# Outer products over all 128 rows and 512 columns, and a new order of the tail, in a decode backward kernel

## The chip, the cores and the metric

The kernel runs on one core of a Trainium2 chip. The metric is the device time of one execution in microseconds; the median of 11 runs of the kernel before is 517.34 us (510.51 to 527.18). Engines are named as in the profile: PE (matmul) and PEld (its weight loads), DVE (vector), ACT (scalar), POOL (GpSimd), SP (which here only issues loads and the two small row stores).

## The reference, cut to what matters

The forward pass is a residual block for one decoded token (batch 2): a layer norm, then grouped-query attention over a cached K and V next to a gated bilinear feed-forward block, both added to x. The kernel returns its output and, by the chain rule, the gradients of x, of both caches and of all weights.

```
x: (2, 1, 576)   k_cache, v_cache: (2, 16, 4096, 128)   wq: (576, 4096)   wo: (4096, 576)
w_gate, w_up: (576, 4608)   w_down: (4608, 576)          all bf16

q = xn @ wq                       # 32 query heads of 128, 2 to each of the 16 key heads
p = softmax(q k^T / sqrt(128));   o = p v;   attention = o @ wo
h = (xn @ w_gate) * (xn @ w_up);  feed-forward = h @ w_down
out = x + attention + feed-forward
returned: out and d/d(x, k_cache, v_cache, wq, wo, w_gate, w_up, w_down) of sum(out * grad_out)
```

The gradients of the caches are sums of two outer products (two query heads to a key head): dV[k, :] = sum over the two heads of p[k] times dO[:], and dK[k, :] the same with the score gradient ds[k] and q[:]. All weight gradients are sums of outer products over the batch of 2. So 92.5 MB are read and 92.5 MB are written, and almost no operand is used twice.

## The kernel before, in words

**Order of the work.** The outer loop has NIT = 16 iterations (L841 to L882): four groups of four key heads, in each group two batches and two pairs s of key heads. One iteration loads two K heads and two V heads (1 MB each) and makes the dV of its own pair and the dK of the pair of the iteration before, which is kept in `last` with its K tiles, its score gradients `dsT`, `dsm` and its queries `bd0`. Each head is one `slot` (L738): its load is issued on SP, then half of the head is transposed on DVE in 32x32 blocks (`t32`, L121, into one of three X tiles) and multiplied on PE by a stationary W (16 matmuls, `head_scores`, L519), then `more(2)` runs two waiting outer-product units, then comes the other half, two more units, and `other(per)`, which runs steps of the list `side`. `side` holds the feed-forward slices (9 slices of 512 columns, `mlp_units`) and, after the last pair of a group, the weight work of the group (`back_units`, L637). `contract` (L535) is the second use of a K or V head: its rows times the probabilities or the score gradients, with the result in `oT`; `end_of_K` and `end_of_V` (L749, L754) call it.

**Outer products of the caches.** `masked` (L557, POOL, 1.9 us) spreads a 128x128 array of probabilities or score gradients into `prm` or `dsm`, eight matrices [128, 128], each with the rows of one part left and the others at zero. `build_bd` (L497) makes the other factor: POOL copies a column of q or dO into the diagonal matrices dM, PE multiplies them by the identity, and ACT copies the result [128, 2 x 128] from PSUM to `bd0` or `bd1` in bf16. `outer_units` (L564) makes eight units of a pair of heads. A unit takes one PSUM tile `ps_o` of two banks (two such tiles exist), fills it with eight matmuls of 32 rows x 128 stationary columns on 128 moving columns, where `32 * a` picks a row strip, and copies its 1024 columns to a quarter of a store tile `so`. The fourth unit of a head issues the store of 1 MB on POOL's queue (L581).

**Who copies out of PSUM.** `evac` (L104) keeps two counters of microseconds, for DVE and ACT, adds its own estimate to the smaller one and so picks the engine; other work is added by hand through `dve()` and `act()`.

**Buffers.** Tag "nat": 12 slots for everything that is loaded (K, V, weights) and, at the end, for the small row tiles of `final_units`. Tag "st": 5 slots for all store tiles but two small ones. Tag "X": 3 slots. `ps_m`, small PSUM tiles: 2.

**The end.** After the loop, `end_of_K` of the last pair runs; then its eight dK units are added to `outs`, and `side` gets, in this order, the small row tiles (`prepare`), `first` (output rows `yp`, the 16 transposes of oT into R, the stationaries of the input gradient), `second` (`dxn`), the rows of out_0 (`output`), `rows` and `gradient` for dx, and then the weight gradients of the last group: `outer_o` (dWo: 8 copies of 576 columns, two stores of 576 KB), `outer_q` (dWq: 4 copies of 1024 columns, two stores of 512 KB) and `outer_qt`. The last loop alternates two dK or dV units with one entry of `side`.

PE runs its instructions in the order in which they were placed; within a `Block` all matmuls follow the first one directly (L83 to L100). The framework places the instructions by priority and adds the semaphores.

Of the kernel before, what the change touches and what calls it, by code (L numbers as in the profile page):

```python
# [11 lines left out]
FP32 = mybir.dt.float32  # L12
BF16 = mybir.dt.bfloat16
P = 128
# [9 lines left out]
def kernel(  # L24
# [201 lines left out]
    oTs = [const.tile([P, 2, GH, 32], BF16, name=f"oT{i}") for i in range(2)]  # L226
    for t in (*Wms, *Wts, *oTs):
        nc.gpsimd.memset(t[:], 0.0)
    nwm = [0]

    rowT = [[const.tile([P, P + 28], BF16, name=f"rowT{t}{i}") for i in range(2)] for t in range(2)]
# [211 lines left out]
    def group_front(g, wq, wo):  # L443
        qd = sb.tile([P, 3, GH, 2], BF16, tag="qd", bufs=2, name="qd")
        qp = ps_m([P, GH, 2])
        with Block() as mm:
            for h in range(GH):
                for dc in range(5):
                    if dc < 4:
                        l, r = wq[:, 2 * dc + h // 4, (h % 4) * P:(h % 4 + 1) * P], xs[:, dc, 0:2]  # L450
                    else:
                        l, r = wq[:, 8, (h % 4) * P:(h % 4 + 1) * P], xs[:, 4 + h // 4, 0:2]
                    mm(qp[:, h, :], lhsT=l, rhs=r, start=(dc == 0), stop=(dc == 4))
        nc.vector.tensor_copy(qd[:, 0], qp[:])
        nc.vector.tensor_scalar(qd[:, 2], qd[:, 0], SCALE, None, op0=ALU.mult)

        do_ps = ps_m([P, GH * 32])
        for half in range(2):
            Xo = xtile([P, GH // 2, D], "Xo")
            t32(pairs(Xo[:].rearrange("p c n -> p (c n)")),  # L460
                pairs(wo[:, 4 * half:4 * half + 4].rearrange("p c n -> p (c n)")))
            with Block() as mm:
                for k in range(NB):
                    for e in range(2):
                        mm(
                            do_ps[:, P * half:P * half + P], lhsT=Wdy[:, k, e, :],
                            rhs=view(Xo[:], 0, P, 64 * k + e, [[D, 4], [2, 32]]),
                            start=(k == 0 and e == 0), stop=(k == NB - 1 and e == 1),
                        )
        dof = sb.tile([P, GH, 32], FP32, tag="dof", bufs=1, name="dof")  # L470
        t32(dof[:].rearrange("p c n -> p (c n)"), do_ps[:])
        nc.vector.tensor_copy(qd[:, 1], dof[:, :, 0:2])


        rp = ps_m([P, 2, 4, GH * 2])
        for t in range(2):
            for be in range(4):
                nc.tensor.matmul(rp[:, t, be, :], lhsT=sel[:, be].rearrange("p a i -> p (a i)"),
                                 rhs=qd[:, t].rearrange("p h b -> p (h b)"), start=True, stop=True)
        rep = sb.tile([P, 2, 4, GH * 2], BF16, tag="rep", bufs=2, name="rep")  # L480
        nc.vector.tensor_copy(rep[:], rp[:])
        dve(2.6 + 1.2)
        return dict(g=g, wq=wq, wo=wo, qd=qd, rep=rep, oT=oTs[g % 2])
# [13 lines left out]
    def build_bd(st, b, s, t):  # L497

        nc.gpsimd.tensor_copy(  # L499
            view(dM[:], 0, P, t * 2 * P, [[P + 2, 2], [4, 32], [1, 2]]),  # L500
            view(st["qd"][:], 0, P, (2 if t == 0 else 1) * GH * 2 + 8 * s + b, [[4, 2], [0, 32], [2, 2]]),
        )
        bp = ps_m([P, 2, Dh])
        for x in range(2):
            nc.tensor.matmul(bp[:, x, :], lhsT=dM[:, t, x], rhs=ident[:], start=True, stop=True)  # L505
        bd = sb.tile([P, 2 * Dh], BF16, tag=f"bd{t}", bufs=2, name=f"bd{t}")
        nc.scalar.copy(bd[:], bp[:].rearrange("p x d -> p (x d)"))
        act(0.4)
        return bd

    def small(name, shape=(P, 1), dtype=FP32, bufs=2):
# [44 lines left out]

    def masked(rows, name):  # L557

        m = sb.tile([P, 8, P], BF16, tag=name, bufs=2, name=name)
        nc.gpsimd.tensor_tensor(m[:], view(rows[:], 0, P, 0, [[0, 8], [1, P]]),  # L560
                                view(maskc[:], 0, P, 0, [[1, 8], [0, P]]), ALU.mult)
        return m

    def outer_units(rows, bd, b, l0, oview):  # L564
        m = {}

        def unit(x, ch, A):
            def f():
                if ch == 0 and A == 0:
                    m["st"] = stile([P, 4, 8, Dh], "so")  # L570
                st = m["st"]
                o = ps_o()
                with Block() as mm:
                    for c in range(4):
                        for aa in range(2):
                            a = 2 * A + aa
                            mm(o[:, aa, c * Dh:(c + 1) * Dh], lhsT=rows[32 * a:32 * a + 32, 4 * ch + c, :],
                                             rhs=bd[32 * a:32 * a + 32, x * Dh:(x + 1) * Dh], start=True, stop=True)
                evac(st[:, 2 * A:2 * A + 2, 4 * ch:4 * ch + 4, :].rearrange("p a c d -> p a (c d)"), o[:], 1024)
                if ch == 1 and A == 1:  # L580
                    nc.gpsimd.dma_start(oview[b, :, :, l0 + x].rearrange("a m n -> m a n"),  # L581
                                        st[:].rearrange("p a c d -> p a (c d)"))
            return f
        return [unit(x, ch, A) for x in range(2) for ch in range(2) for A in range(2)]

    def softmax(s_ps):
        mx = small("mx")
# [49 lines left out]
    def back_units(st):  # L637
        g, wq, wo, oT = st["g"], st["wq"], st["wo"], st["oT"]
        n0 = g * GH * Dh
        m = {}  # L640

        def first():
            yp = ps_m([P, 5, 2])
            with Block() as mm:
                for dc in range(5):
                    for h in range(GH):
                        mm(yp[:, dc, :], lhsT=wo[:, h, DOFF[dc]:DOFF[dc] + P], rhs=oT[:, 0, h, 0:2],
                                         start=(h == 0), stop=(h == GH - 1))
            nc.vector.tensor_add(acc[:], acc[:], yp[:])

            rp = ps_m([P, 2, 2, P], BF16)
            for t in range(2):
                for h in range(GH):
                    a = h // 2
                    nc.tensor.transpose(rp[32 * a:32 * a + 32, t, h % 2, :], oT[:, t, h, :], ident[:])
            m["R"] = R = sb.tile([P, 2, 2, P], BF16, tag="R", bufs=1, name="R")
            nc.vector.tensor_copy(R[:], rp[:])
# [6 lines left out]
            dve(0.2 + 0.5)  # L664

        def second():
            dxn(*m["W"], wq, lambda q, s: (s // 4) * 16 + q * 4 + s % 4, lambda s: s // 4, 2)
# [1 line left out]
        def outer_q(k, A):  # L669
            def f():  # L670
                R = m["R"]
                if A == 0:
                    m["st"] = swtile([P, 2, GH * P], "stq")
                st = m["st"]
                o = ps_o()
                with Block() as mm:
                    for dc in range(2):
                        for aa in range(2):
                            a = 2 * A + aa
                            d0 = (2 * k + dc) * P  # L680
# [23 lines left out]
        def outer_o(A, h2, k):  # L704
            def f():
                R = m["R"]
                if h2 == 0 and k == 0:
                    m["so"] = swtile([P, 4, D], "sto")
                o = ps_o()
                with Block() as mm:  # L710
                    for aa in range(2):
# [6 lines left out]
                    nc.gpsimd.dma_start(out_5[r0:r0 + 4 * P, :].rearrange("(h p) n -> p h n", p=P), m["so"][:])  # L718
            return f

        return [[first], [second], [outer_o(0, 0, 0), outer_o(0, 0, 1)], [outer_o(0, 1, 0), outer_o(0, 1, 1)],
                [outer_o(1, 0, 0), outer_o(1, 0, 1)], [outer_o(1, 1, 0), outer_o(1, 1, 1)],
                [outer_q(0, 0), outer_q(0, 1)], [outer_q(1, 0), outer_q(1, 1)], [outer_qt]]

# [116 lines left out]
    for n in range(NIT):  # L841
# [38 lines left out]
        last = (st, b, s, K, dsT, dsm, bd0)  # L880
        if new:
            st = nxt  # L882
    end_of_K(*last[:5])
    outs += outer_units(last[5], last[6], last[1], G * last[0]["g"] + 2 * last[2], okview)
    units = back_units(last[0])
    side += final[:1] + units[:2] + final[1:] + units[2:]
    while outs or side:
        more(2)
        other(1)
# [30 lines left out]
```

## Time and profile before

| | us |
|---|---|
| median of 11 runs | 517.34 |
| the profiled execution, its own time | 517.05 |
| its span (first to last instruction) | 515.3 |
| PE / DVE / ACT / POOL busy | 422.0 / 353.9 / 332.3 / 201.8 |
| outer matmuls of the caches, 2048, mean 0.24 | 95.1 |
| score matmuls, 2048 | 164.4 |
| ACT copies ps_o to so, 232 of 256, mean 1.02 | 225.2 |
| DVE copies ps_o to so, 24, mean 1.20 | 28.8 |
| POOL masks, 32, mean 1.89 | 60.5 |
| DMA moved | 186.26 MB, 361 GB/s over the span |
| mean granted TensorE clock | 0.831 of full |

How to read it: busy times are per engine and overlap. [...] The page's clock line gives the granted TensorE clock in 40 slices of 12.9 us, in tenths of full speed, the DMA line the busy share of the 16 DMA engines.

### The profile page before, as it was taken

To read this page: it belongs to the slowest core of one execution; us is meant where nothing else is said; L and a number is where in the kernel's file an instruction comes from. 1 tells how busy PE (TensorE), PEld (TensorE's weight loads), DVE (VectorE), ACT (ScalarE), POOL (GpSimd) and SP (SyncE) were. 2 spreads that over 40 slices of the span, in tenths; PEclk is the share of its full clock that TensorE was granted. 3 is DMA by queue.
4 is the path that set the end of the run, shared out by engine and by line. 5 is a ranking of instruction groups with operands and counts; after the bars stand their busy time and mean duration, and the time that the engine had idled before them with its cause. 6 is when DMAs were issued, how large, how long until landed. Compare 5 with 4: busy or idle time off the path is not lost.

```text
span 515.3 us, 20060 instructions
## 1 busy us (share of the span) xinstructions
PE 422.0 (82%) x8921; PEld 338.0 (66%) x8921; DVE 353.9 (69%) x621; ACT 332.3 (64%) x461; POOL 201.8 (39%) x369
## 2 busy tenths in 40 slices
PE   2778997989988987983888889988987988799772
PEld 1667775867776666773677667776776766677630
DVE  6785765556748969563587678768684769598464
ACT  4244795657587486873477864768776475788553
POOL 3224363233352444440534435356243155353313
PEclk9797896577799699986799975889897599999655
DMA  8998999999979999998799999999999999976646
GB/s 257 405 383 315 399 381 386 385 335 390 370 278 406 410 341 415 408 406 347 274 402 398 414 416 396 364 396 417 419 414 392 419 374 379 390 270 234 245 191 238
DMA packets 52911, 186.26 MB, mean 361 GB/s; under 512 B 4140, under 2 KB 19128, under 8 KB 44632
## 3 DMA queue, kind: packets, MB, share of 16 engines
q1 hardware_dynamic: 28392, 92.49, 47.2%
q0 software_dynamic: 24432, 92.48, 45.5%
q8 instruction: 70, 1.15, 0.9%
q14 instruction: 17, 0.14, 0.1%
HBM read 92.48 MB, written 92.48 MB: 359 GB/s over the span
## 4 chain that ended last, share of the span: by engine, by line
PE 53%; ACT 16%; DVE 14%; issue 9%; DMA 4%; SPq 2%; POOL 1%; POOLq 0%; ACTq 0%; DVEq 0%
PE ps_sc L93 20%; PE ps_o L93 14%; ACT so L112 13%; PE ps_m L93 12%; DVE X L121 5%; DMA wd<-in_B_w_down_dram 2%; SPq L313 2%; PE ps_m L554 2%; DVE so L109 2%; DMA wgu<-in_B_w_gate_dram 2%; DVE Xw L121 1%; PE ps_m L603 1%; PE ps_m L625 1%; PE ps_m L505 1%; ACT stw L112 1%
## 5 line engine op out<-in xcount | busy, mean ns | idle before, releaser
L112 ACT CAST so<-ps_o 128x1024 bf16<-128x1024 f32 x232 | 225.2, 1021 | 71.9 <-PE ps_o L93 61.6
L121 DVE STREAM_TRANSPOSE X<-kv 128x1024 f32<-128x1024 f32 x128 | 157.6, 1234 | 51.0 <-PE ps_sc L93 45.6
L93 PE MATMUL ps_sc<-X,W 128*128 128x128 bf16 x2048 | 164.4, 240 | 14.4 <-issue 7.7
L93 PEld LDWEIGHTS <-W 128*128 128x128 bf16 x2048 | 145.9, 108 | 23.2 <-issue 17.4
L581 POOL DMA_DIRECT2D out_dram<-so x64 | 49.9, 779 | 119.2 <-ACT so L112 75.1
L93 PE MATMUL ps_o<-bd,dsm 32*128 32x128 bf16 x1024 | 49.7, 241 | 13.5 <-ACT so L112 9.0
L93 PE MATMUL ps_o<-bd,prm 32*128 32x128 bf16 x1024 | 45.4, 232 | 13.4 <-ACT so L112 5.8
L93 PEld LDWEIGHTS <-dsm 32*128 32x128 bf16 x1024 | 30.5, 102 | 28.4 <-issue 22.8
L93 PEld LDWEIGHTS <-prm 32*128 32x128 bf16 x1024 | 27.5, 98 | 26.1 <-issue 19.3
L93 PE MATMUL ps_m<-kv,rowT 128*32 128x128 bf16 x2048 | 40.8, 240 | 2.6 <-issue 2.0
L112 ACT CAST stw<-ps_o 128x1024 bf16<-128x1024 f32 x28 | 28.0, 1019 | 16.0 <-PE ps_o L93 14.4
L492 POOL COPY W<-rep 32x16 bf16<-32x16 bf16 x128 | 24.8, 194 | 34.1 <-PE ps_sc L93 27.0
L93 PEld LDWEIGHTS <-rowT 128*32 128x32 bf16 x2048 | 34.4, 108 | 5.0 <-issue 2.8
L560 POOL TENSOR_TENSOR prm<-pr,maskc 128x1024 bf16<-128x1024 bf16 x16 | 30.2, 1890 | 15.5 <-DVE pr L608 14.2
L560 POOL TENSOR_TENSOR dsm<-ds,maskc 128x1024 bf16<-128x1024 bf16 x16 | 30.3, 1894 | 9.1 <-DVE ds L628 8.6
L109 DVE CAST so<-ps_o 128x1024 bf16<-128x1024 f32 x24 | 28.8, 1198 | 4.4 <-PE ps_o L93 4.4
L499 POOL COPY dM<-qd 128x128 bf16<-128x128 bf16 x32 | 9.2, 291 | 47.5 <-PE ps_m L505 32.8
L121 DVE STREAM_TRANSPOSE Xw<-wgu 128x1152 f32<-128x1152 f32 x18 | 24.6, 1365 | 4.0 <-PE ps_sc L93 3.9
L112 ACT CAST std<-ps_o 128x576 bf16<-128x576 f32 x36 | 22.1, 646 | 5.9 <-PE ps_o L93 5.1
L112 ACT CAST sto<-ps_o 128x576 bf16<-128x576 f32 x25 | 15.1, 643 | 15.6 <-PE ps_o L93 15.6
L392 POOL DMA_DIRECT2D out_dram<-stw x18 | 13.7, 759 | 29.1 <-ACT stw L112 13.0
L93 PEld LDWEIGHTS <-Wdy 128*128 128x128 bf16 x306 | 22.0, 110 | 4.3 <-DVE Xo L121 2.9
(174 smaller groups left out, 544.5 us busy)
## 6 DMA issues: line engine op xcount, KB each, us to landing
out_dram<-so POOLq DMA_DIRECT2D x64, 1024.0 KB, 11.2
kv<-in_A_k_cache_dram SPq DMA_DIRECT2D x32, 1024.0 KB, 12.7
kv<-in_A_v_cache_dram SPq DMA_DIRECT2D x32, 1024.0 KB, 10.6
out_dram<-stw POOLq DMA_DIRECT2D x18, 512.0 KB, 11.0
wd<-in_B_w_down_dram SPq DMA_DIRECT2D x9, 576.0 KB, 11.3
out_dram<-std POOLq DMA_DIRECT2D x9, 576.0 KB, 8.7
wo<-in_A_wo_dram SPq DMA_DIRECT2D x4, 1152.0 KB, 15.3
wgu<-in_B_w_gate_dram SPq DMA_DIRECT2D x9, 512.0 KB, 17.9
```

The source lines that it names most:

```text
L93: ins = nc.tensor.matmul(*args, **kwargs)
L109: nc.vector.tensor_copy(out=out, in_=in_)
L112: nc.scalar.copy(out, in_)
L121: nc.vector.transpose(out, in_)
L313: nc.sync.dma_start(wgu[64 * w:64 * w + 64, 8], Wsrc[512:576, f0:f0 + FS])
L392: nc.gpsimd.dma_start(out[0:512, f0:f0 + FS].rearrange("(c p) n -> p c n", p=P), st[:])
L492: nc.gpsimd.tensor_copy(view(W[t][:], 32 * a, 32, 28 + 32 * a, [[2 * WW, 4], [WW + 2, 2], [1, 2]]), view(st["rep"][:], 32 * a, 32, t * 4 * ...
L499: nc.gpsimd.tensor_copy(view(dM[:], 0, P, t * 2 * P, [[P + 2, 2], [4, 32], [1, 2]]), view(st["qd"][:], 0, P, (2 if t == 0 else 1) * GH * 2 ...
L505: nc.tensor.matmul(bp[:, x, :], lhsT=dM[:, t, x], rhs=ident[:], start=True, stop=True)
L554: nc.tensor.matmul(t_ps[:], lhsT=o_sb[:], rhs=RV[:].rearrange("p x r -> p (x r)"), start=True, stop=True)
L560: nc.gpsimd.tensor_tensor(m[:], view(rows[:], 0, P, 0, [[0, 8], [1, P]]), view(maskc[:], 0, P, 0, [[1, 8], [0, P]]), ALU.mult)
L581: nc.gpsimd.dma_start(oview[b, :, :, l0 + x].rearrange("a m n -> m a n"), st[:].rearrange("p a c d -> p a (c d)"))
```

## The change

**The factor bd over all rows.** `build_bd` now copies the PSUM result on ACT to a tile `dense`, and POOL copies it, 32 partitions at a time, into the diagonal blocks of one of three permanent tiles `bds` of shape [128, 2, 4, 128], whose other blocks are set to zero once at the start. **The outer units** make 1024 columns in two matmuls of all 128 rows and 512 moving columns each, in place of eight of 32 rows and 128 columns; a unit now covers all four row strips of two of the eight matrices, so its copy writes runs of 128 columns into `so`. `prm` and `dsm` share a tag with three slots (before: two each), and `dof` moves to an X slot. **The tail**: `first` is cut into `output`, `turn(0)`, `turn(1)` and `spread`; the order of `side` changes; two dV units go ahead of the last `end_of_K`; the counters of `evac` restart at zero; the store tiles of the last group's dWo and dWq take "nat" slots.

```diff
+    bds = [const.tile([P, 2, 4, Dh], BF16, name=f"bd{i}") for i in range(3)]
+    for r in bds:
+        nc.gpsimd.memset(r[:], 0.0)
+    n_bd = [0]
...
-        dof = sb.tile([P, GH, 32], FP32, tag="dof", bufs=1, name="dof")
+        dof = sb.tile([P, GH, 32], FP32, tag="X", bufs=3, name="dof")
...
-        bd = sb.tile([P, 2 * Dh], BF16, tag=f"bd{t}", bufs=2, name=f"bd{t}")
-        nc.scalar.copy(bd[:], bp[:].rearrange("p x d -> p (x d)"))
+        dense = sb.tile([P, 2, Dh], BF16, tag="dense", bufs=1, name="dense")
+        nc.scalar.copy(dense[:], bp[:])
         act(0.4)
+        bd = bds[n_bd[0] % 3]
+        n_bd[0] += 1
+        for a in range(4):
+            nc.gpsimd.tensor_copy(bd[32 * a:32 * a + 32, :, a, :], dense[32 * a:32 * a + 32])
         return bd
...
-        m = sb.tile([P, 8, P], BF16, tag=name, bufs=2, name=name)
+        m = sb.tile([P, 8, P], BF16, tag="msk", bufs=3, name=name)
...
-        def unit(x, ch, A):
+        def unit(x, cp):
...
                 with Block() as mm:
-                    for c in range(4):
-                        for aa in range(2):
-                            a = 2 * A + aa
-                            mm(o[:, aa, c * Dh:(c + 1) * Dh], lhsT=rows[32 * a:32 * a + 32, 4 * ch + c, :],
-                                             rhs=bd[32 * a:32 * a + 32, x * Dh:(x + 1) * Dh], start=True, stop=True)
-                evac(st[:, 2 * A:2 * A + 2, 4 * ch:4 * ch + 4, :].rearrange("p a c d -> p a (c d)"), o[:], 1024)
-                if ch == 1 and A == 1:
+                    for c in range(2):
+                        mm(o[:, c, :], lhsT=rows[:, 2 * cp + c, :], rhs=bd[:, x].rearrange("p a d -> p (a d)"),
+                           start=True, stop=True)
+                evac(view(st[:], 0, P, 2 * cp * Dh, [[Dh, 2], [8 * Dh, 4], [1, Dh]]),
+                     o[:].rearrange("p c (a d) -> p c a d", a=4), 1024)
+                if cp == 3:
...
+        stq = nat if g == NGRP - 1 else swtile
...
-                    m["st"] = swtile([P, 2, GH * P], "stq")
+                    m["st"] = stq([P, 2, GH * P], "stq")
...
-                    m["so"] = swtile([P, 4, D], "sto")
+                    m["so"] = stq([P, 4, D], "sto")
...
-        return [[first], [second], [outer_o(0, 0, 0), outer_o(0, 0, 1)], [outer_o(0, 1, 0), outer_o(0, 1, 1)],
+        return [[output, lambda: turn(0), lambda: turn(1), spread], [second], [outer_o(0, 0, 0), outer_o(0, 0, 1)], [outer_o(0, 1, 0), outer_o(0, 1, 1)],
...
+    load["v"] = load["s"] = 0.0
+    units = back_units(last[0])
+    o_first, q_first = units[0][:2], units[0][2:]
+    side += final[:1] + [o_first] + final[1:2] + units[2:4]
+    more(2)
     end_of_K(*last[:5])
     outs += outer_units(last[5], last[6], last[1], G * last[0]["g"] + 2 * last[2], okview)
-    units = back_units(last[0])
-    side += final[:1] + units[:2] + final[1:] + units[2:]
+    side += [q_first, units[1]] + final[2:] + units[4:]
```

`output` holds the matmuls of `yp` and their addition to acc; `turn(t)` transposes the eight heads of one half of oT into half of R, through a PSUM tile of its own; `spread` holds the four matmuls with `sel` and the stationaries. Their instructions are those of `first`, with two copies into R in place of one.

More of the change, by code (lines that the diff above doesn't have):

```diff
@@ L565, in outer_units @@
         m = {}
-        def unit(x, ch, A):
+        def unit(x, cp):
             def f():
-                if ch == 0 and A == 0:
+                if cp == 0:
                     m["st"] = stile([P, 4, 8, Dh], "so")
@@ L583, in unit @@
             return f
-        return [unit(x, ch, A) for x in range(2) for ch in range(2) for A in range(2)]
+        return [unit(x, cp) for x in range(2) for cp in range(4)]
     def softmax(s_ps):
@@ L640, in back_units, with output @@
         m = {}
-        def first():
+        stq = nat if g == NGRP - 1 else swtile
+        def output():
             yp = ps_m([P, 5, 2])
@@ L649, in first, with turn, spread @@
             nc.vector.tensor_add(acc[:], acc[:], yp[:])
[L651 to L657, printed above, removed]
+            dve(0.2)
+        def turn(t):
+            if t == 0:
+                m["R"] = sb.tile([P, 2, 2, P], BF16, tag="R", bufs=1, name="R")
+            rp = ps_m([P, 2, P], BF16)
+            for h in range(GH):
+                a = h // 2
+                nc.tensor.transpose(rp[32 * a:32 * a + 32, h % 2, :], oT[:, t, h, :], ident[:])
+            nc.vector.tensor_copy(m["R"][:, t], rp[:])
+            dve(0.3)
+        def spread():
             rp = ps_m([P, 32, 2])
@@ L663, in first @@
             m["W"] = stationaries(rp[:], lambda h: (P * h, [[1, P]]))
-            dve(0.2 + 0.5)
         def second():
```

## The prediction

> **What bounds the kernel now.** I read the page's shares first, then its 40 slices, then a table of stages (busy time by engine, granted TensorE clock, DMA share), then the instructions in order of time at two places.
>
> ```profile
> span 515.3 us, 20060 instructions
> PE 422.0 (82%) x8921; PEld 338.0 (66%) x8921; DVE 353.9 (69%) x621; ACT 332.3 (64%) x461; POOL 201.8 (39%) x369
> ...
> PEclk9797896577799699986799975889897599999655
> DMA  8998999999979999998799999999999999976646
> ```
>
> No engine is full, the DMA engines nearly are until slice 36, and the clock line keeps falling to 5. The stages (columns: stretch; length, then busy us and instruction count of PE, weight load, DVE, ACT, POOL; granted clock, DMA share, GB/s) show three states:
>
> ```profile
> 82.00:102.40 20.40, 19.69 (x279) 15.82 (x279) 11.48 (x21) 13.65 (x18) 7.17 (x17) 0.50 1.04 401
> 146.80:167.30 20.50, 18.42 (x474) 14.78 (x472) 14.81 (x24) 14.86 (x20) 7.44 (x18) 1.00 1.01 396
> 450.60:478.00 27.40, 24.92 (x600) 19.97 (x597) 24.15 (x41) 23.84 (x33) 11.99 (x15) 1.00 0.69 260
> 479.40:498.40 19.00, 14.82 (x239) 9.15 (x236) 8.39 (x17) 9.73 (x11) 3.40 (x6) 0.55 0.59 224
> 498.40:510.90 12.50, 6.13 (x42) 1.57 (x35) 9.72 (x16) 6.42 (x9) 4.44 (x7) 0.50 0.60 222
> ```
>
> (1) At half clock (82 to 102) PE is full and does 279 matmuls where a full-clock stretch does 474: PE is the bound. (2) At full clock with loads running, DMA is (1.01). (3) After the loads, at 450 to 478, DVE and ACT are both near 88%; from 479 to the end nothing is full, DMA runs at 0.6, the clock is 0.5, and ACT waits for PE and PE for ACT. The clock is at half for 34% of the span (mean 0.831).
>
> Now one pair of outer units and a score batch, at full clock (first two rows) and at half (last two):
>
> ```profile
> 445.05 0.42 PE L93 MATMUL ps_o<-bd,prm 32*128 32x128 bf16 x16
> ...
> 445.41 1.09 PE L93 MATMUL ps_sc<-X,W 128*128 128x128 bf16 x16
> ...
> 86.56 1.87 PE L93 MATMUL ps_sc<-X,W 128*128 128x128 bf16 x16 [0.23 <-DVE X L121]
> ...
> 88.36 0.63 PE L93 MATMUL ps_o<-bd,dsm 32*128 32x128 bf16 x16
> ```
>
> Sixteen 32-row matmuls hold PE only 0.36 us (445.05 to 445.41)[...]. Sixteen 128-row matmuls take 1.09 us at full clock and 1.87 at half.
>
> **What sets the clock.** I counted, for each 3.413 us step of the clock record, the matmul columns that started in it, each weighted by the part of the array it covers (128x128 as 1; 32x128 and 128x32 as a quarter), as a share of the 8192 columns[...]. The clock of the next step is full where the share is at least 0.37 and half where it is below, in 138 of 146 steps; weights of 1 miss 21. From the matmul counts by shape: 82 to 102 holds 80 score matmuls and 96 outer ones, with the rest about 15,600 of 49,152 columns, 0.32; 146.8 to 167.3 holds 118 and 95, with the rest 0.54.
>
> [...] PE is 97% busy by the profile at 82 to 102 and stays at half[...]. [...] the trace has 147 ns from the last outer matmul start to the first score matmul at 445.4, against 57 ns between score matmuls. [...] the page's slices reach 419, and I use 415. [...]
>
> **The change, part by part.** The sum is made against the profiled 517.05 us: a span of 515.3 and 1.75 around it. The median shown, 517.34, is 0.3 above.
>
> *PE time of the outer units.* 256 units of 8 matmuls (2048 in all) become 256 of 2. A 512-column matmul isn't in the trace; four times the 57 ns spacing of 128 columns is 0.23 us[...]. The trace has 57 undivided pairs, the rest mostly single since the second ps_o buffer was not free: 57 x 0.41 = +23 us of PE time. Bounds: 0 (all single) and 128 x 0.41 = +52[...].
>
> *The clock.* A unit's area goes from 256 full columns to 1024. Put into the steps of before (12 units at 82 to 102: 0.32 + 12 x 768/49,152 = 0.51), it brings the steps below 0.37 from 34% to 17%. 499 of 2048 score matmuls ran cold: 31 batches at 1.87 - 1.09 = 0.78 are 24 us; the 464 cold contraction matmuls (7 of 32 sets, 1.90 against 1.08) 6; other work about 17: 47 us of PE time if nothing is cold, half of it, -24, by the count. So PE's total hardly moves (-1), but it is taken away where PE is the bound and added where ACT, DVE or DMA is. At 450 to 478 the period of a half slot is two ACT copies (2 x 1.02), and PE needs 0.92 + 0.86 for it: just hidden; without that cover it is +0.4 a half slot.
>
> *What that is worth.* From 5 to 450 us 170 MB move; at 415 GB/s that is 410 us, so 35 us of DMA idleness is there to be won, most of it after cold stretches (140 to 145: share 0.35; 240 to 250: 0.58 and 0.38). I take 6; bounds -16 and +10.
>
> *POOL.* Each of 32 builds adds four 32-partition copies of 256 elements. The rows W (16 elements, 194 ns) and dM (128, 291 ns) give 0.87 ns an element: 0.40 us each, 1.6 a build, 51 us in all; POOL goes from 39% to 49%. Behind them in the same queue stand the masks, build_W and all store issues, and the copies wait there for ACT's copy to dense, so they can hold a store longer than 1.6. It is hidden by the five st slots: 107 stores are one each 4.8 us, so a slot may live 24 us; it lives about 11.2 (landing) + 5 (filling) + 2 (queue) = 18. Cost 0; if that cover is gone, up to 51. Three memsets of 1024 elements at the start (about 1 us each by the row of 1248, 1.14) precede PE's first matmul: 0. Sharing msk (3 for 4 slots) and three bd buffers: each old user is done half an iteration earlier: 0. dof in an X slot: four extra rotations among 171: 0. The ACT copy to dense is the old one. The evacuation has the same 1024 columns in runs of 128, as stw has (1019 ns against 1021 for so): 0.
>
> *The tail.* Moved: the output rows, R's first half, out_0 and four of the eight sto evacuations with their store (one POOL issue) go between the key units; the second half of R, the stationaries, dxn and the gradient (its dx store on SP, which has no loads left) go after them. The two balancing counters restart at zero, so evacuations alternate; before, 11 of 14 so copies fell to ACT. The last sto and stq tiles no longer wait for st. From 479.4 to 510.9 ACT has 16.2 us of work and DVE 18.1: 34.3, or 17 if shared evenly. PE must feed it: 14 units of 0.43 to 0.5 at full clock are 7 us, other matmuls about 5. Stores still to move are 7.9 MB (224 and 222 GB/s over those stretches and the landing), 19 us at 415. I take 21.5 in place of 31.5: -10. Bounds -14 (17 us) and 0 (the hand-over between PE and the evacuating engine stays the limit, with the last steps cold).
>
> Sum: 515.3 - 6 - 10 = 499; with what lies around it **501 us**.
>
> **Rivals.** A: *the clock is full nearly everywhere*. Speaks for it: 0.51 is far above 0.37. The steady part nears 415 GB/s: -16 and -11, 490 us. Against: loads also wait on slots for reasons other than PE. B: *it is hidden anyway*. In the loaded part DMA is at 1.0, and a tail of short hand-overs gains only a little: 517 (512 to 522). C, slower: *POOL's queue holds the stores*. Place: the four copies after each build, ahead of a finished so tile. For: POOL's longest waits are for ACT, and a copy that waits for dense stops all behind it. Against: 61% of POOL is idle and the evacuations wait only 3.1 us in all for a landing. It decides from the point where a tile's life grows by over 6 us (18 to 24); with 3 us passed on in half of 32 builds, less the tail's gain, 517 + 24 - 10 = 531. D: *the clock does not answer*, as three quarters of the new stationary work multiplies zeros: +23 of which some two thirds on the path, no gain in the tail: 532. The trace shows nothing of zeros.
>
> **How the numbers follow.** Forecast 0.49 (its own range 493 to 510), A 0.15, B 0.16, C 0.12, D 0.08. Faster by over 1% (below 512; 1% is about what a measurement of this kernel can tell): 0.64; within: 0.16; slower: 0.20. Leaving out about 0.08 below and 0.12 above, the range is 488 to 528.
>
> **What would show it.** Outer matmuls 128*128 with 512 columns, 512 of them, about 0.22 us apart; mean clock at 0.90 or above and no half-clock stretch of 20 us; DMA near 1.0 with fewer dips; POOL at about 250 us with waits for dense; so copies shared by ACT and DVE after 479; last store issued 20 to 23 us after the last contraction. Wrong, if the clock stays near 0.83, if evacuations wait for out_dram by tens of us, or if the tail from the last load to the end is still 65 us.

## The result, and the profile after

| | us |
|---|---|
| after, median of 12 executions | 523.08 (519.36 to 526.15) |
| before, on the same chip, median of 47 | 516.89 (508.02 to 527.18) |
| ratio after / before | 1.020, 95% interval 1.017 to 1.0235 |
| forecast | 501 (488 to 528) |

Slower, by 1.2% by the medians and by 2.0% by the ratio: the forecast had the wrong sign, though the range holds the time. Ratios here compare only the executions within 1.5% of each kernel's fastest on one chip; the kernel before spreads more widely than the changed one, so the ratio stands above the quotient of the medians.

The page after, the same rows as of before:

```profile
span 522.9 us, 17085 instructions
PE 425.4 (81%) x7307; PEld 308.8 (59%) x7385; DVE 352.1 (67%) x625; ACT 334.8 (64%) x461; POOL 254.0 (49%) x500
...
PEclk9898999879998899978878998599899997999985
DMA  8999999999799999994996899799998999887557
...
L516 POOL COPY bd<-dense 32x256 bf16<-32x256 bf16 x128 | 50.7, 396 | 18.1 <-ACT dense L511 13.6
```

The clock line has lost nearly all its 5s and 6s (mean 0.909, before 0.831), and PE's busy time is about what it was (this trace has records of 434 of the 512 wide matmuls; their weight loads are all there). But the DMA line now has a 4 and a 6 in the middle (slices 19 and 22), where the line of before has nothing under 7. POOL has its 51 us.

The stages, in the stretches of the prediction and then the end (columns: stretch; length, busy us and count of PE, weight load, DVE, ACT, POOL; clock, DMA share, GB/s):

```profile
82.00:102.40 20.40, 14.31 (x240) 10.58 (x242) 10.99 (x21) 13.87 (x19) 10.60 (x24) 0.94 1.04 405
146.80:167.30 20.50, 18.26 (x302) 13.78 (x303) 18.19 (x32) 12.89 (x20) 8.92 (x20) 0.94 1.03 410
450.60:478.00 27.40, 26.28 (x433) 19.90 (x439) 21.52 (x37) 22.43 (x31) 20.25 (x40) 1.00 0.80 302
488.80:508.80 20.00, 13.84 (x160) 6.42 (x160) 11.84 (x18) 12.43 (x15) 6.77 (x11) 0.94 0.68 258
508.80:518.50 9.70, 6.60 (x35) 1.96 (x33) 7.65 (x16) 5.65 (x8) 3.20 (x6) 0.50 0.78 286
```

At 82 to 102 PE is no longer full and the clock is 0.94 in place of 0.50: it rose with the added columns, as forecast. But DMA was at 1.04 there before as well (401 GB/s, now 405), so that stretch had little to gain. What was lost later is seen in the times of the 16 softmax maxima (one an iteration): the eighth comes at 256.5 us, 5.4 earlier than before (261.9), the ninth at 300.2, 5.9 later than before (294.3), and the last at 476.7 against 467.1. The stretch between the eighth and the ninth took 43.6 us in place of 32.4; that between the seventh and the eighth took 39.2, before 39.8. DMA idleness, summed over 5 us steps from 5 to 450, is 25.2 us; before it was 16.0. ACT waits 15.4 us in all for landings of stores, before 3.1.

The DMA line's 4 comes just ahead of that stretch. The stages there, of after (first fence) and of the kernel before (second):

```profile
225.00:241.00 16.00, 7.42 (x53) 5.27 (x53) 4.72 (x10) 5.48 (x9) 1.16 (x2) 0.76 0.86 336
241.00:250.00 9.00, 8.42 (x226) 6.48 (x227) 5.07 (x10) 5.66 (x10) 8.14 (x14) 0.87 0.44 136
250.00:262.00 12.00, 6.30 (x97) 4.42 (x96) 7.42 (x10) 4.77 (x8) 4.11 (x8) 0.79 1.00 387
```

```profile
225.00:241.00 16.00, 10.45 (x167) 8.30 (x165) 6.78 (x10) 9.61 (x14) 2.62 (x7) 0.82 1.05 410
241.00:250.00 9.00, 5.51 (x158) 4.74 (x158) 4.45 (x12) 3.37 (x6) 4.37 (x4) 0.54 0.41 123
250.00:262.00 12.00, 9.50 (x198) 7.95 (x199) 9.32 (x14) 6.20 (x11) 4.08 (x6) 0.86 1.01 410
```

The kernel before has the same hole in its transfers at 241 to 250 (0.41 against 0.44). In the changed kernel it begins earlier (0.86 against 1.05 at 225 to 241), so that DMA is idle for 7 of these 37 us, before for 4. The instructions in order of time, of POOL, of ACT and of DVE, show the queues there (in brackets the idle time before an instruction and what ended it):

```profile
240.60 1.89 POOL L568 TENSOR_TENSOR prm<-pr,maskc 128x1024 bf16<-128x1024 bf16 x1 [13.91 <-DVE pr L615]
242.45 1.69 POOL L516 COPY bd<-dense 32x256 bf16<-32x256 bf16 x4
...
234.46 0.39 ACT L511 CAST dense<-ps_m 128x256 bf16<-128x256 f32 x1
...
238.58 1.38 DVE L121 STREAM_TRANSPOSE Xd<-wd 128x1152 f32<-128x1152 f32 x1 [6.42 <-DMA wd<-in_B_w_down_dram]
...
240.13 0.32 DVE L615 TENSOR_SCALAR pr<-ex,rz 128x128 bf16<-128x128 f32 x1
```

`dense` was ready at 234.85, but its copies began at 242.45: ahead of them in POOL's queue stood the mask of pr, pr stood in DVE's queue behind the transposition of wd, and that waited 6.42 us for a load. (In the kernel before DVE has the same order and waits 6.27 us for wd, but there ACT's one copy made the operand, and POOL's mask held nothing of it.) So this operand was ready 9.3 us late, at 244.1. The next outer units do not need it, though. The first matmul that reads it comes 20 us later:

```profile
264.33 0.61 PE L93 MATMUL ps_o<-bd,dsm 128*128 128x512 bf16 x1
```

This holds throughout: in the changed kernel each of the 32 operands lies finished for at least 6.9 us, 14 in the median, before the first weight load of the units that read it, and PE and its weight loads wait 0.7 us in all for operands and masks. Over the 32 builds, from the first build matmul to the end of the last write to the operand:

| kernel | median us | sum us | longest |
|---|---|---|---|
| before | 1.1 | 43 | 2.3 |
| after | 4.8 | 184 | 13.1 |

Rival C of the prediction feared for the stores. From the last copy into an so tile to its issue they took 50.4 us over 64 stores (longest 3.7), before 41.9 (longest 4.8): little is held there. But they bunch. No store is issued from 225.93 to 247.24; then five follow up to 255.26, and these take all five st tiles. ACT's next copy waits for the first of them to land, PE for ACT's copy, DVE for PE's next score matmuls:

```profile
247.24 0.79 POOL L588 DMA_DIRECT2D out_dram<-so  x1
...
260.26 1.93 ACT L112 CAST so<-ps_o 128x1024 bf16<-128x1024 f32 x2 [5.05 <-DMA out_dram<-so]
261.32 1.01 PE L93 MATMUL ps_o<-bd,prm 128*128 128x512 bf16 x2 [4.92 <-ACT so L112]
...
267.11 1.25 DVE L121 STREAM_TRANSPOSE X<-kv 128x1024 f32<-128x1024 f32 x1 [9.15 <-PE ps_sc L93]
```

This is at the head of the stretch that took 11 us longer, and DMA runs empty twice behind it (0.41 and 0.44; the kernel before is at 1.02 in both):

```profile
275.00:280.00 5.00, 4.84 (x83) 4.19 (x84) 2.08 (x5) 3.62 (x6) 3.05 (x4) 0.76 0.41 161
285.00:290.00 5.00, 4.83 (x122) 4.02 (x121) 4.75 (x11) 4.55 (x7) 3.62 (x13) 1.00 0.44 128
```

### The profile page after: what moved, and what is told of

Its sections match the earlier page's. It is cut to its first block, busy times and chain, and to the rows that moved or that the text cites. A ratio compares the mean times of both kernels' runs of the same rounds, so it can differ in the third digit from the quotient of the medians.

```text
span 522.9 us, 17085 instructions
## 1 busy us (share of the span) xinstructions
PE 425.4 (81%) x7307; PEld 308.8 (59%) x7385; DVE 352.1 (67%) x625; ACT 334.8 (64%) x461; POOL 254.0 (49%) x500
## 4 chain that ended last, share of the span: by engine, by line
PE 46%; ACT 17%; DVE 14%; DMA 14%; issue 6%; SPq 2%; POOL 0%; POOLq 0%; ACTq 0%; DVEq 0%
PE ps_sc L93 15%; PE ps_o L93 15%; ACT so L112 13%; PE ps_m L93 12%; DMA out_dram<-so 5%; DVE X L121 5%; DMA out_dram<-sto 3%; DMA kv<-in_A_k_cache_dram 3%; DMA wd<-in_B_w_down_dram 2%; SPq L317 2%; DVE so L109 1%; PE ps_m L562 1%; DVE Xw L121 1%; ACT sto L112 1%; PE ps_m L632 1%
## 5 line engine op out<-in xcount | busy, mean ns | idle before, releaser
L112 ACT CAST so<-ps_o 128x1024 bf16<-128x1024 f32 x231 | 225.0, 1018 | 84.5 <-PE ps_o L93 44.4
L93 PE MATMUL ps_sc<-X,W 128*128 128x128 bf16 x2048 | 146.7, 225 | 7.3 <-DVE X L121 6.3
L93 PEld LDWEIGHTS <-W 128*128 128x128 bf16 x2048 | 132.9, 100 | 23.0 <-issue 10.4
L93 PE MATMUL ps_o<-bd,prm 128*128 128x512 bf16 x216 | 69.2, 403 | 12.7 <-ACT so L112 8.5
L93 PE MATMUL ps_o<-bd,dsm 128*128 128x512 bf16 x218 | 68.5, 392 | 9.2 <-ACT so L112 3.2
L516 POOL COPY bd<-dense 32x256 bf16<-32x256 bf16 x128 | 50.7, 396 | 18.1 <-ACT dense L511 13.6
L109 DVE CAST so<-ps_o 128x1024 bf16<-128x1024 f32 x25 | 30.1, 1204 | 14.1 <-PE ps_o L93 11.4
L93 PEld LDWEIGHTS <-prm 128*128 128x128 bf16 x256 | 21.6, 101 | 28.3 <-issue 17.8
L93 PEld LDWEIGHTS <-dsm 128*128 128x128 bf16 x256 | 21.5, 99 | 24.9 <-issue 15.0
L93 PEld LDWEIGHTS <-xnr 32*128 32x128 bf16 (+1 forms) x440 | 13.6, 96 | 23.6 <-issue 18.5
L559 ACT COPY o_sb<-ps_m 128x128 f32<-128x128 f32 x32 | 8.7, 270 | 24.7 <-PE ps_m L93 24.1
```

Of the source, the lines that this page charges most:

```text
L93: ins = nc.tensor.matmul(*args, **kwargs)
L109: nc.vector.tensor_copy(out=out, in_=in_)
L112: nc.scalar.copy(out, in_)
L516: nc.gpsimd.tensor_copy(bd[32 * a:32 * a + 32, :, a, :], dense[32 * a:32 * a + 32])
L559: nc.scalar.copy(o_sb[:], o_ps[:])
```

## The experiments

All times are medians; beside each group of runs the kernel before was executed too (516.9 to 517.7). "Old end" is the kernel before's `back_units` and last lines. The letters of the theories are those of the expectations; each group of runs has its own.

**The change cut in parts.** Three theories: P, POOL's copies hold the stores in its queue; M, the longer matmuls hold PE's queue; T, the new end loses. First the end alone, on the kernel before: its `back_units` and the lines after the loop are those of the changed kernel.

> The kernel before with the tail's edits alone (the cut first, the new order of side, two units ahead of the last contraction, counters at zero, nat slots for the last store tiles); outer products as before. Before: 517; the change: 523. Theory T (the new tail costs the 6 us): 522 to 524. Theories P and M (the loss is made before the tail): 510 to 517, a gain of up to 7, since the time from the last maximum to the end is 46.2 us after the change against 48.2 before it.

Measured 528.4, ratio 1.020 (1.012 to 1.027), clock 0.81. So the end's edits do lose, but not at the end: in the profile the last maximum is at 485.7 (before 467.1), while from there to the end it takes 43.8 us (before 48.2). The end gains 4 us, and what comes ahead of it loses 19. T named the edits, but not the place nor the size (522 to 524).

Second, the changed kernel with the old end.

> The change with the tail of before: 512-column outer products, bd tiles filled by POOL, msk and dof as in the change. Theory T: 515 to 518. Theories P (POOL's copies hold the stores) and M (the longer matmuls hold PE's queue): 523 to 527.

Measured 520.1, ratio 1.0105 (1.007 to 1.014), clock 0.92: between the ranges of the theories.

Third, only POOL's part: dense, the four copies, the shared tags, but the old end and the old eight matmuls, which now read their blocks out of the wide operand:

```
-   rhs=bd[:, x].rearrange("p a d -> p (a d)")          # two of 128 rows
+   rhs=bd[32 * a:32 * a + 32, x, a, :]                 # eight of 32 rows
```

> POOL's part alone: bd tiles filled by the four POOL copies of each build, msk and dof as in the change, but the outer products as eight matmuls of 32 rows and 128 columns that read the diagonal blocks; tail of before. PE's instructions and array area are then those of before. Theory P: 521 to 526, most of the loss is here. Theory M: 516 to 518, POOL's 51 us are hidden by its idle time.

Measured 528.3, ratio 1.021 (1.015 to 1.028), clock 0.82. So POOL's part costs 11 us with the old matmuls, over P's range by 2, and the longer matmuls then give 8 back (528.3 to 520.1): M is refuted. That POOL's part loses is as P said; that it does so by holding the stores is not shown by this.

Fourth, the second without POOL's copies and ACT's copy: one DVE product of the PSUM result with a mask of four row strips (Q4) writes the wide operand.

```
-   nc.scalar.copy(dense[:], bp[:]);  four nc.gpsimd.tensor_copy(bd[32a.., :, a, :], dense[32a..])
+   nc.vector.tensor_tensor(bd[:], bp over 4 strips, Q4 over 2 x 128, ALU.mult);  dve(1.2)
```

> PE's part without POOL's copies: 512-column outer products, each bd tile made by one DVE product of the PSUM result with a 0/1 row mask (1024 elements, about 1.2 us, 38 us more on DVE in all) in place of ACT's copy and POOL's four; tail of before. Theory P: 512 to 518, at or below before. Theory M: 522 to 528, as slow as the change, and a little more for DVE.

Measured 512.2, ratio 0.9985 (0.996 to 1.001), 8 us below its twin with POOL's copies.

**The same in the changed kernel itself**: the DVE product in place of the two kinds of copies, all else as changed.

> The changed kernel (523.1 us) with one thing undone: the operand is made by one DVE product, without ACT's copy to dense and POOL's four copies. Theory P (POOL's copies carry the change's loss, the new end does nothing without them): 509 to 513. Rival E (the new end loses 3 us or more by itself in the changed kernel): 514 to 518.

Measured **506.9**, ratio 0.980 (0.9755 to 0.985), clock 0.93: below the ranges of both theories. With this one part undone the change is 2% faster than the kernel before, so the path through ACT's and POOL's copies costs 16 us more than the DVE product (by the medians; 4% by the ratios). The new end, which cost 3 us with POOL's copies (520.1 to 523.1) and 11 on the kernel before, gains 5 here (512.2 to 506.9). The same stages in this kernel's profile:

```profile
225.00:241.00 16.00, 10.38 (x185) 7.96 (x182) 8.38 (x15) 9.94 (x15) 5.95 (x10) 0.85 1.03 410
241.00:250.00 9.00, 6.62 (x141) 4.51 (x142) 3.56 (x7) 3.80 (x6) 1.89 (x1) 0.69 1.02 419
250.00:262.00 12.00, 11.37 (x187) 7.87 (x185) 11.81 (x20) 8.72 (x11) 4.01 (x7) 1.00 1.04 379
```

DMA stays at 1.02 and above where both other kernels fall to 0.4. Here DVE has pr ahead of the transposition of wd. The operand takes 1.7 us in the median (74 in all, longest 8.8), DMA idleness is 11.7 us, and the stores wait 30.7 us in all from the last copy to the issue.

**Are the end's units the loss, since all four groups use them?** On the kernel with the DVE product and the old end (512.2): only the new units, in all groups, in the old order of the end; then the whole new end, with the old first unit in the first three groups.

> The kernel with the DVE product (512.2 us) plus only the new back_units: the first unit of each of the four head groups is cut into output rows, two turns and the spread, and the last group's tiles lie in load slots; the order of the last steps is the old one. Theory S (the tail edits lose in the middle, since back_units serves all four groups): slower than 512.2 by 3 to 8 us, 515 to 520, with the loss in the iterations after each change of group. Rival E (the new end itself loses): 512 within 1.5 us.

> The kernel with the DVE product (512.2 us) plus the whole new end (counters at zero, new order, load slots), but with the old first unit for the first three groups. Theory S: no loss in the middle and 1 to 4 us won at the end, 508 to 511. Rival E: the loss of the end shows, 515 to 520.

Measured 510.6 (ratio 0.988, 0.982 to 0.994) and 511.8 (0.993, 0.991 to 0.996). The first is not slower by 3 to 8 us, as S said; the second is not at 515 to 520, as E said. Both fall: neither part of the end loses anything where POOL's copies are gone.

**Stores off POOL's queue**: the so stores issued by ACT, with POOL's copies (old end) and with the DVE product.

> The kernel with the new outer products, POOL's copies and the old end (520.1 us), but the so stores are issued from ACT's queue in place of POOL's. Theory H (POOL's copies cost time because finished so tiles wait behind them in POOL's queue): the stores no longer stand behind them, so this kernel comes within 3 us of its twin without POOL copies and with the same store queue. Rival N (the copies cost by themselves: the operand comes later, POOL's other work is late, the shared buffers hold): the difference of 8 us between the twins stays, 6 to 10 us. Alone, H expects about 512, N about 520, each moved by whatever ACT's queue does to both twins.

> The twin: the kernel whose cached operand is made by one DVE product with no POOL copies (512.2 us), with the so stores issued from ACT's queue. It only shows what the queue itself does: both theories expect 512 within 5 us; under H its distance to the kernel with POOL copies and ACT stores is under 3 us, under N 6 to 10 us.

Measured 562.3 and 560.8. The twins are 1.6 us apart, as H said, but they stand 42 and 49 us above their versions with POOL's stores, far from what both theories expected of either, so another limit may hide the copies. Inconclusive.

**Which property of the copies?** On the kernel with the DVE product and the old end (512.2), four POOL copies a build into a scratch tile that nobody reads. First from a constant, so that they wait for nothing:

> The kernel with the DVE product and the old end (512.2 us), plus the four POOL copies of 32 x 256 a build, from a constant into a scratch tile that nobody reads: they wait for nothing. Theory O (POOL's occupancy by itself costs, 51 us more on POOL): about 520, 518 to 523. Theories H (the copies' wait for the operand holds what stands behind them in POOL's queue) and L (the operand itself comes later to PE): 512 within 2 us.

Measured 546.8 (ratio 1.055), a miss for all: since they waited for nothing, the framework put 123 of the 128 into the first 75 us, where they hold up POOL's other work. One row of POOL from this run:

```profile
39.36 13.04 POOL L518 COPY scr<-ident 32x256 bf16<-32x256 bf16 x29
```

The second maximum is at 92.7 in place of 58.9; from there on both kernels take the same time (453.2 and 452.0 us). Repeated with the copies tied to their place behind dM:

> The kernel with the DVE product and the old end (512.2 us), plus four POOL copies a build that wait for nothing and are tied to their place behind the build's dM copy. Theory O (occupancy of POOL by itself costs): 517 to 521. Theory H (only a copy that waits holds the stores): 512 within 2 us.

Measured 513.8, ratio 1.0005 (0.998 to 1.0035): POOL's occupancy as such costs 1.6 us here; O is refuted. With copies that read the finished operand and so wait for it:

> The same, but the four POOL copies read the finished operand and so wait for it, as the change's copies wait for dense; PE does not wait for them. Theories O and H: about 520, 518 to 523. Theory L: 512 within 2 us. With the run before: O is 520 and 520, H 512 and 520, L 512 and 512.

Measured 516.7, ratio 1.002 (0.999 to 1.005): 4.5 us, between the theories. The same in the changed kernel's own frame, on 506.9:

> The changed kernel with the DVE product for the operand (506.9 us), plus four POOL copies a build that read the finished operand and that nobody waits for: the same POOL time and the same kind of wait in POOL's queue as the change has, but the operand is not late. Theory L (it is the operand's lateness that costs): 505 to 511. Theory H (waiting copies hold POOL's queue): 518 to 524.

Measured 513.9, ratio 0.998 (0.995 to 1.000). Again between: of the 16 us, 7.0 return with copies that wait in POOL's queue though nobody reads them, and 9.2 more (to 523.1) when the operand itself goes through dense and these copies. The three ratios (0.980, 0.998, 1.020) have intervals that do not meet. The last step also puts ACT's copy back and takes the product (32 of about 1.2 us) from DVE, so the 9.2 us are not the operand's alone. The queue's part is seen in POOL's waits of this run (total us, times, longest):

```profile
POOL scr L518 <- DVE bd L514: 21.9, 17, 2.6
```

**Is it the order of the queues?** A rule added to the changed kernel, to the kernel before and to the one with the DVE product: the transposition of wd may not be placed ahead of the last pr.

```
+   with tc.issue_after(last_pr.ins):
        t32(Xd, wd)
```

> The changed kernel (523.1 us), POOL's copies kept, with one rule of order: DVE's transposition of wd to Xd is never queued ahead of the last pr. Theory Q (the loss is the order: pr behind Xd's wait for its load, POOL's mask behind pr, copies and stores behind the mask): 506 to 513. Theory K (the copies themselves cost, wherever they stand): 519 to 525.

> The kernel before (517.1 us) with the same rule of order. Theory Q expects it to gain as well, since its own DVE queue has Xd ahead of pr in the middle: 508 to 514. Theory K says nothing of it: 517 within 3 us.

> The changed kernel with the DVE product in place of ACT's and POOL's copies (506.9 us) and the same rule of order. Theory Q: its order is nearly so already, 503 to 508, and the distance to the changed kernel with the rule and with copies is under 4 us. Theory K: 507 within 2 us, and that distance is 12 us or more.

Measured 520.1 (ratio 1.007, 1.0025 to 1.011), 517.4 and 509.3. The rule makes the changed kernel 3 us faster (1.4% by the ratios), does not help the kernel before (its ratio is 1.006, 1.002 to 1.009) and makes the third 2 us slower; 11 of the 16 us stay between the first and the third. Q is refuted as the main cause; K, which expected 12 or more between them, is nearly right. The operands of the first still take 4.8 us. Last, the second build of an iteration emitted ahead of the mask of pr, and no mask placed ahead of earlier copies:

> The changed kernel (523.1 us) with POOL's copies on the operand's path, but the second build of an iteration is emitted before the mask of pr, and a mask is never queued ahead of the copies emitted before it: the copies no longer stand behind the mask's wait for pr. Theory L: the time from the build's matmuls to the finished operand falls from 4.8 us in the median to 3 or less, and the kernel to 510 to 517. Theory H or K: 519 to 525, whatever the operand's time.

Measured 520.2, ratio 1.011 (1.005 to 1.018). The operand's time fell to 3.1 us (122 in all, longest 12.4), nearly as L wanted, but the kernel gained only 3 us (0.9% by the ratios) and stays in the range of H and K: L's 510 to 517 is missed. Part of the wait was turned round, since now the mask stands behind the copies and these wait for ACT's dense. The two kernels' waits, this run first:

```profile
POOL bd L517 <- ACT dense L512: 27.9, 18, 4.9
...
POOL prm L570 <- DVE pr L617: 3.9, 1, 3.9
```

```profile
POOL prm L568 <- DVE pr L615: 34.2, 13, 13.9
...
POOL bd L516 <- ACT dense L511: 13.6, 7, 6.2
```

Nor is the mask's wait a loss by itself: in the kernel with the DVE product and the old end (512.2) it is 38.5 us in 13 waits, longer than in the changed kernel:

```profile
POOL prm L566 <- DVE pr L613: 38.5, 13, 12.2
```

**Is the clock worth its own price?** On the kernel before, one more full matmul of 512 columns ahead of each unit's eight, overwritten by them: array area and nothing else.

```
+   mm(o[:, 0, :], lhsT=rows[:, 4 * ch, :], rhs=rows[:, 0:4, :] as 512 columns, start=True, stop=True)
```

> The kernel before (517.1 us) with one more 128x128 matmul of 512 columns at the head of each of the 256 outer units, whose result the eight row matmuls overwrite: array area without any other change of the change. Theory C (the clock is worth what the 37 executions of the kernel before show, 2.0 us for 0.01): the clock rises from 0.83 to 0.90 or more, PE gets 56 us of matmuls more, and the time still falls, 503 to 514. Rival W (a high clock goes with short times but does not make them, and PE's added time counts): 520 to 540 at the higher clock.

Measured 540.9, ratio 1.037 (1.029 to 1.045). The clock rose as forecast (0.83 to 0.92), PE's busy time too:

```profile
PE 476.4 (89%) x9177; PEld 338.1 (63%) x9177; DVE 352.4 (65%) x621; ACT 336.6 (63%) x461; POOL 200.5 (37%) x369
```

W holds, with a time 1 us over its range: 256 fillers of about 0.22 us (two wide matmuls of the changed kernel start 0.215 apart) are 56 us, PE's time from each start to the next (at most 0.45 us counted for each matmul) rose from 449 to 490, and this costs more than the clock returns. Among the 37 executions of the kernel before that ran beside the first four kernels, a clock higher by 0.01 goes with 2.0 us less, but that does not make it the cause.

## Why the prediction was wrong, step by step

**The clock: right.** In the clock records of before and after every stretch but the last is a whole number of steps of 3.413 us (36 and 26 stretches), and the granted share is 1.0 or 0.5. The prediction's count, full clock after a step with a share of 0.37 or more, was found on the trace before (8 misses in 146 steps); it fits the trace after as well (4 misses in 147 steps, with the wide matmuls that it recorded) and that with the DVE product, where all are recorded (2 in 142). Its 8192 columns a step are a unit of the count: at the 0.215 us of a wide matmul at full clock, 8128 start in a step. The share of half-clock time fell from 34% to 19% (17% was forecast), cold score matmuls from 499 to 172, the mean clock came to 0.909. **What bounded it: read too simply.** The prediction called PE the bound at 82 to 102, but its own line has DMA at 1.04 there, as full as in its case (2), and after the change the stretch moves 405 GB/s in place of 401.

**PE time of the outer units: about right.** Two wide matmuls in a row, for the spacing:

```profile
497.10 0.59 PE L93 MATMUL ps_o<-bd,dsm 128*128 128x512 bf16 x2
```

One takes 0.377, so the second starts 0.215 later; that is the median of 229 such gaps at full clock, and 0.424 that of 24 at half. A pair of units is then 4 x 0.215 = 0.86 us and a unit alone 0.43. In the trace before a pair took 0.36, and the first score matmul started 0.147 after the pair's last one, 0.09 more than the 0.057 between score matmuls. 0.86 - 0.36 - 0.09 is the prediction's 0.41 a pair; a unit alone, 0.33 and 0.09 before, comes out even. From each matmul's start to the next, at most 0.45 us for each, the outer ones went from 98 to 126 us (130 with the DVE product, whose trace lacks none of them), so +28 to +32 where +23 was forecast; the score ones from 158 to 134 (-24), the cache contractions from 40 to 39, the rest from 153 to 146; the sum from 449 to 445.

**Worth in the loaded part, -6: of the right order once POOL is out of it.** With the DVE product the last maximum is at 460.1, 7.0 earlier than before; with the DVE product and the old end it is at 465.3, only 1.8 earlier, so the agreement with 6 is in part luck. The 35 us of idleness that were to be won from are 16.0 by the DMA share.

**POOL, "Cost 0": this is the step that failed.** Count and size were right (128 copies of 396 ns, 50.7 us), and so was "they can hold a store longer than 1.6" as a worry. But the prediction put the whole at nothing, since five store slots would hide it, and it cost 16.2 us: from 506.9 with the DVE product to 523.1 (in the profiles the last maximum moves from 460.1 to 476.7). Of this the busy time is little (1.6, measured with the old end); 7.0 come back with copies that wait in POOL's queue and that nobody reads; how the other 9.2 arise stays open.

The cover of the slots was worked out as if stores came evenly, one each 4.8 us, so that a tile might live 24 us and lives 18. In the trace after they bunch, five in 8 us after 21 without one, and ACT waits 15.4 us in all for landings (before 3.1; with the DVE product ACT and DVE wait 9.3 together). So the slots do not always cover, but these waits are not the sum of the loss either. The prediction also did not ask who waits for what the copies produce, and there the lateness looks like the answer: the operand's time went from 1.1 to 4.8 us in the median, and up to 13.1. The trace speaks against it as a direct cause: every operand is finished at least 6.9 us before its first use, and shortening the time to 3.1 gave only 3 us.

**The rest at 0**: memsets, msk, bd, dof and the copy's new pattern were not tried singly. All of them are in the kernel with the DVE product, which is faster, so no large loss shows there. The so copy took 1018 ns, as forecast.

**The tail, -10: mis-sized.** From the last V contraction's end to the last store's issue it took 30.4 us (488.8 to 519.15) against 31.5; from the last maximum to the end 46.2 against 48.2, and 45.3 with the DVE product: -2.9 of -10. The forecast shared the copies evenly and let PE feed them at full clock. DVE took 6 of the 17 so copies (before 3 of 14), but the hand-over stayed, and at 508.8 the clock was at half again (0.50 to 518.5; by the count the share of the steps is at most 0.11 from 506.2 on): the last units have 32 rows, and the rows of dx and their DVE chain now stand there. Three stretches of the order of time, of PE, of ACT and of DVE:

```profile
508.34 2.29 PE L813 MATMUL ps_o<-accx,F 128*2 128x160 f32 x8
...
511.03 2.49 ACT L112 CAST sto<-ps_o 128x576 bf16<-128x576 f32 x4 [1.94 <-PE ps_o L93]
...
515.06 0.75 DVE L841 TENSOR_TENSOR dx_bf<-t,dy_f 2x576 bf16<-2x576 f32 x1
515.74 1.21 DVE L109 CAST stq<-ps_o 128x1024 bf16<-128x1024 f32 x1
```

Eight f32 matmuls for the rows of dx hold PE for 2.29 us while ACT waits, and one of the last stq copies stands behind the dx chain on DVE. 7.9 MB still had to move at 258 to 286 GB/s, not 415.

**The rivals.** C had the sign and the engine. Its time of 531 is 8 us too long, and by its own terms it would be further off: 3 us in half of 32 builds are 48, not 24, so nearness in the time is luck. Its mechanism is not shown: from the last copy to the issue the so stores took 50.4 us in all against 41.9 before and 30.7 with the DVE product, which is 0.3 us a store. The 7.0 us of the copies that wait and that nobody reads come nearest to it. A and B do not apply; D is refuted by the clock.

**What stays open.** How the path through POOL turns into 16 us: neither the operand's lateness nor the mask's wait does it by what PE waits for, and the parts of the 7.0 us that fall to masks, stores and other work on POOL were not separated. Every edit also makes the framework place all queues anew (POOL's mask and stores changed places between the kernels), so a difference of a few us can be one of placement; that rival was not tested. What stands against it is that the copies lose in each of three frames (528.3 against 517.1, 520.1 against 512.2, 523.1 against 506.9), though the first compares them with ACT's one copy. Why the new end costs 11 us on the kernel before, most of it in the middle and at a lower clock, 3 with POOL's copies and gains 5 with the DVE product is open too: units and order, tried apart, do not tell.

## What to carry to other kernels

When a step of an operand's making is moved to another engine, its busy time alone is no price: here 51 us of copies cost 1.6 us where they waited for nothing, 4.5 and 7.0 where they waited in the queue and nobody read them, and 16 as the way of the operand itself. Nor is a late operand a loss by itself: look up when it is first read, before the wait is called the cause. A stretch that looks bad in the changed kernel must be looked up in the kernel before as well; the hole at 241 to 250 is in both. A higher granted clock paid here where it came with PE work that was wanted (the wide matmuls gave 8 us, at 0.92 in place of 0.82), and not where it came with filler matmuls (24 us lost, at 0.92 in place of 0.83). Try the product that writes the operand in one pass from PSUM before a copy and a spread over two engines: with it this change gives 506.9 us, faster than both kernels.

## What the runs showed of the hardware that was not expected

A so store (1 MB) takes 0.77 us of POOL's queue to issue, and 0.38 us of ACT's, yet issued from ACT they made the kernel 42 to 49 us slower in both twins; in the second a copy on ACT waited 6.94 us for a landing (until 310.77) and the next store came behind it at 314.84; the cause of the rest was not followed further. The wide matmuls count in full for the clock in the trace after (4 misses in 147 steps; weighed at a quarter of their area they make 29), although three quarters of bd, their moving operand, are zeros: with them it rose to 0.91, and with the filler matmuls, which work on masked rows alone, to 0.92.
